# Large transfers of a two-layer SSM and MLP gradient kernel moved to other places in their queues

## The chip, the cores and the metric

The kernel runs on one core of one Trainium2 chip. A core has five engines that run their own instruction streams in order: PE (matrix multiplies; PEld is its weight load), DVE (vector), ACT (scalar and table functions), POOL and SP. Transfers between the device memory and the on-chip memory are issued by SP, ACT and POOL, each into a queue of its own, and are carried by 16 DMA engines that all queues share. SP does nothing in this kernel but issue transfers.

The metric is the time of one launch on the device in microseconds. Five runs of the kernel before gave 790.87 to 794.15 us, median 792.38 us.

## The reference, cut to what matters

The sequence has S = 2048 positions and D = 448 features, the inner width of the dense block is F = 1792, and all data are bfloat16. The kernel returns the output and eight gradients.

```
def A(q, k, v, shift_k, ssm_k, ssm_D):          # SSM convolution block
    kv = causal_conv4(k, shift_k) * v
    y  = irfft(rfft(kv, 4096) * rfft(ssm_k, 4096))[:2048] + kv * ssm_D
    return q * y
def B(x, w1, w2):                               # dense block
    return silu(x @ w1) @ w2

x = A_q
for layer in (0, 1):
    x = x + A(layernorm(x), A_k, A_v, A_shift_k, A_ssm_k, A_ssm_D)
    x = x + B(layernorm(x), B_w1, B_w2)
# outputs: x, and the gradients of sum(x * grad_out) with respect to
# A_q, A_k, A_v, A_shift_k, A_ssm_k, A_ssm_D, B_w1, B_w2
```

The convolution's result y does not depend on the layer, so it is computed once. The gradient that reaches y is summed over both layers and then goes back through the convolution once.

## The kernel before, in words

The program has three stages. `_ssm_prefix` computes y with a Fourier transform of 4096 points that is written as matrix products (a stage with the table M1, a transpose, a stage with a small table, and the inverse with the table Minv), and stores the spectra of the filter and of kv to the device memory (`SPEC_d["K"]`, `SPEC_d["KV"]`). `Main.run` does both layers forward and the dense blocks backward. `_ssm_suffix` takes the gradient back through the convolution and computes the gradients of the weights.

`Main.run` works on four chunks of 512 positions. Its first loop is the forward pass of layer 0. Its second loop does, for each chunk, layer 1 forward and backward; its third loop does layer 0 backward. For one chunk and half of F (seven tiles of 128), `h` makes the hidden activations `aT` (SiLU) and keeps the pre-activations `dT`, from which `slope` makes the derivative on ACT, in place, seven tiles in four instructions. `out` multiplies by w2 (`ps_o`). `ga` computes the gradient of the hidden layer in seven steps: `ps_g` on PE, a copy `ghp` on ACT out of PSUM, and a product with `dT` on DVE, which gives `ghT`. PSUM has two buffers for `ps_g`, so PE can be two steps ahead of ACT's copies and no more. `gn` multiplies by w1 (`ps_n`) and goes back through both layer norms, token tile by token tile: a copy `lb_u` on ACT, then a chain of vector instructions on DVE.

In layer 0, `dT` is stored to the device memory (`DT_d`) and is read back for the backward pass by `load_d` (L690), into tiles `dTl` of 896 KB that share three buffers with `dT`. The last chunk of the second loop loads the first one (`d0`), then `d1` and `e0`; the third loop loads the rest, each right after a transpose.

For the weight gradients, positions have to lie on the partitions, so `aT` and `ghT` are turned by transposing transfers from SP (`store_turned`, L484, two for each half of F, into a tile `turned` with two buffers) and the turned tiles are stored to `A_d` and `GH_d` by L486. That store is kept back in `self.late` until the next turn, and waits until its transposes have landed. Four blocks of layer 0's activations are stored untransposed in `AP_d` and are turned later by `turn_plain` (L496), in the second loop, one for each chunk.

`_ssm_suffix` starts with `_fft_stage1` (`ps_s` <- `gYb`, `M1s`; sixteen steps, copies `A1g` on ACT or DVE), then transposes (`ps_tr`), then seven spectrum steps of 2048 columns. In such a step `spectrum(cp)` loads the pieces of both stored spectra (`kk_c`, two buffers used in turn: K and KV, 512 KB each, from POOL's queue), transforms (`ps_s` <- `Zg`) and swaps halves by two transfers from ACT's queue (`xsw_c`, 256 KB each); `inverse(cp)` makes the products `pa` and `pb` on DVE and runs the inverse matmuls `ps_v`. `spectrum(cp + 1)` is issued ahead of `inverse(cp)`.

The weight gradients are 28 jobs each for w2 and w1: `_job` loads one `dstat` of 512 KB from SP's queue (L776) and does 16 matmuls `ps_d` with it against a big tile that stays: X and `GO` (grad_out) for w2, `mov3` and `mov1` for w1. These matmuls depend on little else, and the framework's scheduler lays them between the instructions of the other stages. The first three jobs' `dstat` are loaded while layer 0's backward pass starts.

The order of instructions on each engine is written out by the framework's scheduler when the program is built. `high_priority` brings an instruction forward, and `issue_after(x)` holds what is issued under it behind x. A tile with a `tag` shares its memory with the others of that tag in a pool, and waits for the release of the one before it. Tags that the change touches are: `WA` (w1sb, then `GO`), `WB` (w2sb, then `mov3`), `Y` (Ysb, then `ksf`), `GY` (gYb, then `gks`), and `kk0` (M1s, then every second `kk_c`). The big tiles are 1792 KB each (`GO`, `mov3`, `ksf`, `gks`); the tables `M1s` and `Minvs` are 1024 KB each.

Of the kernel before, what the change touches and what calls it, by code (L numbers as in the profile page):

```python
# [11 lines left out]
BF16 = mybir.dt.bfloat16  # L12
# [5 lines left out]
P = 128  # L18
# [3 lines left out]
J = 16  # L22
# [226 lines left out]
def _pm(ap2d):  # L249
    return ap2d.rearrange("(p j) d -> p j d", j=J)  # L250
# [213 lines left out]
class Main:  # L464
# [97 lines left out]

    def h(self, c, L, nT, half, hold):
        nc, k = self.nc, self.k
        aT = self.td.tile([P, NF // 2, 512], BF16, name="aT", tag="T", bufs=3)
        dT = self.td.tile([P, NF // 2, 512], BF16, name="dT", tag="D", bufs=3)
        hold.append((aT, dT))
        for ft0, n, at in ((0, 2, 1), (2, 2, 0), (4, 2, None), (6, 1, None)) if half == 0 else ((7, 1, None), (8, 2, 1), (10, 2, 0), (12, 2, None)):
            ps = k.psum.tile([P, 2, 512], FP32, name="ps_h", tag="mm", bufs=2)
            self.contract(ps, self.w1sb, nT, ft0, n, at)  # L570
            o = ft0 - 7 * half
            a = aT[:, o:o + n, :]
            tm = dT[:, o:o + n, :]
            last = nc.scalar.activation(a, ps[:, 0:n, :], ACT.Silu)  # L574
            e = nc.scalar if o == 4 else nc.vector
            _copy(nc, e, tm, ps[:, 0:n, :])
            k.bal.add("act", 0.52 * n)
            k.bal.add(*(("act", 0.52 * n) if e is nc.scalar else ("dve", 0.6 * n)))
        if L == 1:
            if half == 1:  # L580
                with self.tc.issue_after(last.ins):
                    for _, d in hold:
                        self.slope(d)
        else:
            nc.gpsimd.dma_start(out=k.DT_d[c, half], in_=dT[:])
            self.store_turned(k.A_d[0], aT, c, half, ((0, 4), (4, 7)) if half == 0 else ((4, 7),))
            if half == 1:
                nc.gpsimd.dma_start(out=k.AP_d[:, :, 512 * c:512 * (c + 1)].rearrange("ft f s -> f ft s"), in_=aT[:, 0:4, :])
        if L == 1:
            self.store_turned(k.A_d[1], aT, c, half)  # L590

    def out(self, c, aT, last):
# [114 lines left out]
    def run(self):  # L707
# [21 lines left out]
        for c in range(4):  # L729
            gb, gT = self.g_pre(c, 1)  # L730
            self.h(c, 1, nT, 1, cur)
            if c < 3:
                na1 = self.a_fwd(c + 1, 2, None)
            self.out(c, cur, True)
            self.turn_plain(c)
            if c == 3:
                d0 = self.load_d(0, 0)
                self.slope(d0)
                k.GO = k.wk.tile([P, NT, D], BF16, name="GO", tag="WA")
                with self.tc.issue_after(k.d_load.ins):  # L740
                    nc.sync.dma_start(out=k.GO[:], in_=_pm(k.grad_out[0]))
            box = []
# [6 lines left out]
            else:  # L749
                d1, e0 = self.load_d(0, 1), self.load_d(1, 0)  # L750
                k.go_jobs = k.d_load
                nl = self.load_n(0)
# [3 lines left out]
        for c in range(4):  # L756
# [10 lines left out]
            if c < 3:  # L767
                with self.tc.issue_after(k.d_load.ins):
                    nl = self.load_n(c + 1)
        self.flush()  # L770

# [52 lines left out]
def _ssm_suffix(k):  # L824
# [7 lines left out]
    with ExitStack() as es:  # L832
        pool = lambda name: es.enter_context(tc.tile_pool(name=name, bufs=1, reuse_waits="tile"))
        sp0 = pool("sp0")
        k.M1sb = sp0.tile([P, 16, 2, P], BF16, name="M1s", tag="kk0")
        with tc.high_priority():
            nc.gpsimd.dma_start(out=k.M1sb[:].rearrange("p a c k -> p (a c k)"), in_=k.m1_h.ap())
        sp = pool("sspec")
# [3 lines left out]
        Z = sp.tile([P, NDH, P], BF16, name="Zg")  # L842
        k.mov3 = k.wk.tile([P, NT, D], BF16, name="mov3", tag="WB")
        ksf = k.yk.tile([P, J, D], BF16, name="ksf", tag="Y")
        B1k = A1[:].rearrange("p a c n s -> p (a c n s)").rearrange("p (q d) -> p q d", d=D)
        _load_minv(k, nc.gpsimd)
        for n2 in range(16):
            _fft_stage1(k, n2, k.gYb[:, n2, :], A1, psum)
        with tc.tile_pool(name="sspec2", bufs=1, reuse_waits="tile") as p1:
# [8 lines left out]
            def spectrum(cp):  # L858
# [4 lines left out]
                nc.gpsimd.dma_start(out=t[0], in_=k.SPEC_d["K"][:, lo:hi])  # L863
                nc.gpsimd.dma_start(out=t[1], in_=k.SPEC_d["KV"][:, lo:hi])
                if cp == 4:
                    nc.gpsimd.dma_start(out=k.mov3[:], in_=_pm(k.N_d[3][:]))
                if cp == 2:
                    nc.gpsimd.dma_start(out=ksf[:], in_=_pm(k.KS_d[:]))
                for u in range(2):
# [8 lines left out]
            def inverse(cp, t):  # L878
                for u in range(2):
                    ci = 2 * cp + u  # L880
                    o = slice(u * 1024, (u + 1) * 1024)
                    for spec_t, B1, cnd in ((t[1], B1k, True), (t[0], Z, False)):
# [5 lines left out]
                        _fft_inv_stage2_chunk(k, pa, pb, True, B1, ci, psum, cnd=cnd)  # L888

            prev = spectrum(0)  # L890
            for cp in range(NCI // 2):
# [4 lines left out]
        p2 = es.enter_context(tc.tile_pool(name="sp2", bufs=1, reuse_waits="tile"))  # L896
        gks = k.xg.tile([P, J, D], BF16, name="gks", tag="GY")
        gkh = p2.tile([P, 3, D], BF16, name="gkh")
        kx = p2.tile([P, 19, D], BF16, name="kx_s")
        nc.gpsimd.memset(kx[0:1, 0:3, :], 0.0)  # L900
        for h in range(2):
            sl = slice(8 * h, 8 * h + 8)
            nc.scalar.dma_start(out=gks[:, sl, :], in_=v_pm[:, sl, :])
        nc.scalar.dma_start(out=kx[:, 3:19, :], in_=k_pm)
# [126 lines left out]
```

## Time and profile before

The profiled execution took 791.43 us with a span of 789.6 us on the core, at a mean granted PE clock of 0.978. The median of the five runs is 0.95 us above it.

| what | before |
|---|---|
| median of 5 runs | 792.38 us |
| profiled execution, its span | 791.43 us, 789.6 us |
| PE busy | 723.1 us, 92% of the span |
| DVE, ACT, POOL busy | 65%, 56%, 13% |
| moved by DMA | 183.69 MB, mean 233 GB/s |
| stages, from the span's start | prefix to 104 us, layer 0 forward to about 232, layer 1 to 408, layer 0 backward to 527, suffix to the end |

In the profile's lines "L574" is a line of the kernel, "out<-in" names the tiles with the buffer numbers left out, and "SPq", "ACTq" and "POOLq" are the instructions that issue transfers. What stands behind "<-" in square brackets is the instruction whose end closed an engine's idle time; it is inferred from semaphores. The stages' borders above are read from the timeline of PE. The view of waits gives us in total, the number of times and the longest; the view by windows gives for each stretch its length, each engine's busy time (with instructions), the granted PE clock, the DMA engines' busy share, which can exceed 1 a little, and GB/s.

### The profile page before, as it was taken

The numbers are of one execution on the slowest core, as the hardware profiler recorded it, in microseconds if no ns is written. First come the engines' busy times: TensorE is split into PE (matmuls) and PEld (weight loads), VectorE is DVE, ScalarE is ACT, GpSimd is POOL, SyncE is SP. The second block draws the span as 40 slices with busy tenths as digits, with TensorE's granted clock in tenths as the row PEclk, the third lists the DMA queues.
The fourth block names the chain that finished last, engine by engine and source line by source line (L and its number), as shares of the span: only waits on it lengthen the run. The fifth ranks groups of instructions, "written<-read, shape, count | busy, mean of one in ns | idle before, by whom it ended". The sixth has DMA issues, their size and how long they took to land.

```text
span 789.6 us, 12745 instructions
## 1 busy us (share of the span) xinstructions
PE 723.1 (92%) x5025; PEld 379.4 (48%) x5025; DVE 515.3 (65%) x1056; ACT 440.6 (56%) x551; POOL 102.6 (13%) x169
## 2 busy tenths in 40 slices
PE   5999779999999999999987898996979999999995
PEld 4976434444443444434433443343556774545553
DVE  3789678788434977859457877986455625797110
ACT  4879777666566576876846766643536644000000
POOL 1133212222100000000000000010111123111111
PEclk9999899999999999999998999998989999999998
DMA  9359999999977879879997987996978776687650
GB/s 307 147 158 283 372 234 310 306 268 208 241 217 140 178 194 218 214 171 219 352 274 229 237 226 202 262 213 202 413 218 265 249 267 218 181 304 223 189 178 17
DMA packets 188889, 183.69 MB, mean 233 GB/s; under 512 B 135483, under 2 KB 164031, under 8 KB 187805
## 3 DMA queue, kind: packets, MB, share of 16 engines
q1 hardware_dynamic: 173664, 120.93, 59.3%
q0 software_dynamic: 12832, 53.92, 19.6%
q10 hardware_dynamic: 2332, 8.03, 3.3%
q8 instruction: 39, 0.64, 0.3%
q14 instruction: 22, 0.17, 0.1%
HBM read 76.50 MB, written 65.87 MB: 180 GB/s over the span
## 4 chain that ended last, share of the span: by engine, by line
PE 32%; DVE 20%; issue 18%; ACT 14%; DMA 11%; POOL 4%; SPq 0%; POOLq 0%; DVEq 0%; ACTq 0%
PE ps_o L598 6%; PE ps_h L518 6%; PE ps_d L778 5%; ACT ghp L625 3%; DVE dT L113 3%; PE ps_g L518 2%; DMA dTl<-DT_d 2%; PE ps_n L666 2%; DVE lb_junk L641 2%; DVE ghT L630 2%; DMA kk_c<-spec_KV 2%; PE ps_v L232 2%; PE ps_v L233 2%; DVE lb_u L652 2%; DMA turned<-ghT 2%
## 5 line engine op out<-in xcount | busy, mean ns | idle before, releaser
L778 PEld LDWEIGHTS <-dstat 128*128 128x128 bf16 x896 | 86.5, 99 | 85.5 <-issue 6.4
L518 PE MATMUL ps_g<-gT,w2T 128*128 128x512 bf16 (+1 forms) x448 | 100.7, 386 | 15.8 <-ACT ghp L625 15.2
L518 PE MATMUL ps_h<-nT,w1sb 128*128 128x512 bf16 (+1 forms) x448 | 103.9, 385 | 4.9 <-DVE dT L113 2.6
L666 PE MATMUL ps_n<-w1T,ghT 128*128 128x448 bf16 x448 | 93.2, 353 | 1.2 <-DVE ghT L630 0.3
L598 PE MATMUL ps_o<-w2sb,aT 128*128 128x448 bf16 x448 | 90.8, 353 | 0.7 <-ACT aT L574 0.7
L778 PE MATMUL ps_d<-mov,dstat 128*128 128x448 bf16 x448 | 87.2, 352 | 1.1 <-DMA mov<-N_d 1.1
L574 ACT ACTIVATE aT<-ps_h 128x1024 bf16<-128x1024 f32 (+1 forms) x64 | 58.3, 918 | 37.3 <-PE ps_h L518 28.8
L113 DVE CAST dT<-ps_h 128x1024 bf16<-128x1024 f32 (+1 forms) x56 | 59.3, 1065 | 25.9 <-ACT aT L574 25.6
L625 ACT CAST ghp<-ps_g 128x1024 bf16<-128x1024 f32 x56 | 56.5, 1009 | 30.5 <-DVE ghT L630 19.2
L518 PEld LDWEIGHTS <-w2T 128*128 128x128 bf16 (+1 forms) x448 | 36.3, 97 | 76.7 <-issue 46.2
L518 PEld LDWEIGHTS <-w1sb 128*128 128x128 bf16 (+1 forms) x448 | 36.3, 97 | 68.5 <-issue 40.5
L666 PEld LDWEIGHTS <-ghT 128*128 128x128 bf16 x448 | 41.6, 98 | 46.2 <-DVE ghT L630 5.8
L598 PEld LDWEIGHTS <-aT 128*128 128x128 bf16 x448 | 42.1, 98 | 43.3 <-issue 4.3
L778 PE MATMUL ps_d<-X,dstat 128*128 128x448 bf16 x224 | 53.6, 369 | 4.2 <-DMA dstat<-A_d 4.2
L804 ACT COPY do<-ps_dt 112x512 bf16<-112x512 bf16 x14 | 8.2, 586 | 82.6 <-PE ps_dt L802 82.6
L232 PE MATMUL ps_v<-Gsb,pa 128*128 128x128 bf16 x336 | 42.8, 221 | 9.8 <-DVE Zg L113 5.5
L778 PE MATMUL ps_d<-GO,dstat 128*128 128x448 bf16 x224 | 49.5, 353 | 0.0
L233 PE MATMUL ps_v<-Gsb,pb 128*128 128x128 bf16 x336 | 41.7, 221 | 1.4 <-DVE pb L443 1.2
L819 DVE CAST dout<-ps_d 128x448 bf16<-128x448 f32 x14 | 8.7, 622 | 51.4 <-PE ps_d L778 51.4
L232 PEld LDWEIGHTS <-pa 128*128 128x128 bf16 x336 | 33.2, 99 | 12.2 <-DVE pa L442 6.5
L668 ACT ACTIVATE lb_u<-ps_n,rstd 128x448 f32<-128x448 f32 x32 | 20.3, 633 | 33.1 <-DVE X L653 12.1
L630 DVE TENSOR_TENSOR ghT<-dT,ghp 128x1024 bf16<-128x1024 bf16 (+1 forms) x32 | 19.5, 619 | 27.6 <-ACT ghp L625 27.6
(188 smaller groups left out, 1184.2 us busy)
## 6 DMA issues: line engine op xcount, KB each, us to landing
GH_d<-turned SPq DMA_DIRECT2D x16, 896.0 KB, 5.6
dstat<-A_d SPq DMA_DIRECT2D x28, 512.0 KB, 6.6
dstat<-GH_d SPq DMA_DIRECT2D x28, 512.0 KB, 3.8
A_d<-turned SPq DMA_DIRECT2D x12, 896.0 KB, 4.8
DT_d<-dT POOLq DMA_DIRECT2D x8, 896.0 KB, 6.4
dTl<-DT_d SPq DMA_DIRECT2D x8, 896.0 KB, 6.3
spec_K<-Z POOLq DMA_DIRECT2D x7, 512.0 KB, 7.7
KB<-Z POOLq DMA_DIRECT2D x14, 256.0 KB, 12.0
```

The source lines that it names most:

```text
L113: eng.tensor_copy(out, in_)
L232: nc.tensor.matmul(pv[:, i, :], lhsT=pa[:, i * P:(i + 1) * P], rhs=k.Gsb[:, ga, :], start=True, stop=False)
L233: nc.tensor.matmul(pv[:, i, :], lhsT=pb[:, i * P:(i + 1) * P], rhs=k.Gsb[:, gb, :], start=False, stop=True)
L518: self.nc.tensor.matmul(ps[:, u, :], lhsT=w[lo:hi, b, f:f + P], rhs=x[lo:hi, b, :], start=(seen[u] == 1), stop=(seen[u] == ND))
L574: last = nc.scalar.activation(a, ps[:, 0:n, :], ACT.Silu)
L598: nc.tensor.matmul(po[:, :D], lhsT=aT[ft // 7][0][:, ft % 7, tl * P:(tl + 1) * P], rhs=self.w2sb[:, ft, :], start=(ft == 0), stop=(ft == N ...
L625: k.last_gh = nc.scalar.copy(gh[:], ps[:])
L630: nc.vector.tensor_tensor(out=ghT[hh][:, o:o + len(u), :], in0=dT[hh][1][:, o:o + len(u), :], in1=gh[:, u[0]:u[0] + len(u), :], op=ALU.mult)
L641: nc.vector.scalar_tensor_tensor(out=junk[:], in0=u0, scalar=1.0, in1=n_t, op0=ALU.mult, op1=ALU.mult, accum_out=cp[:, 1:2])
L666: nc.tensor.matmul(pn[:, :D], lhsT=ghT[ft // 7][:, ft % 7, tl * P:(tl + 1) * P], rhs=self.w1T[:, ft, :], start=(ft == 0), stop=(ft == NF - 1))
L668: last_u = nc.scalar.activation(u0[:], pn[:, :D], ACT.Identity, scale=k.rstd[2 * L + 1][:, t:t + 1], accum_out=cp[:, tl, 0:1])
L778: i = k.nc.tensor.matmul(ps[:, :D], lhsT=st[:, t, :], rhs=mov[:, t, :], start=start and t == 0, stop=stop and t == NT - 1)
```

## The change

Nothing is computed differently. Transfers change their place, their queue, their number of pieces or their buffer.

- `d0`, the first `dTl`, is loaded at the start of `h(3, 1, ..., 1)` through the new argument `pre`, and no longer after `out(3)`. In SP's order it now stands behind the transposes of chunk 2's last `ghT` and ahead of chunk 3's last transposes. Its slopes move in ACT's order from behind chunk 3's activations to between chunk 2's `lb_u` copies.
- `turn_plain` runs twice in chunks 0 and 1 of the second loop, and not in chunks 2 and 3.
- `GO` is loaded in chunk 0 of the third loop, behind `load_n(1)`, and no longer in chunk 3 of the second.
- `M1s` is loaded by SP in chunk 2 of the third loop, into the tag `WB`, and no longer by POOL at high priority into `kk0`. `kk0` is then free for `kk_c` from the start.
- `mov3` had been loaded on POOL as soon as w2sb was free; it now follows `M1s` in `WB` and is loaded behind the spectra of step 5.
- `Minvs`, `ksf` and `gks` are loaded on POOL behind the spectra of steps 2, 3 and 4. `gks` had been two transfers on ACT's queue behind stage 1, and is now one.

As the scheduler sees other ready times, the order on PE, DVE, ACT and POOL changes too between about 355 us and the end of the spectra: the copies and matmuls of stage 1 start among layer 0's last `ps_n`, and the two `kk_c` pairs of steps 0 and 1 come ahead of the other large loads.

```
-    def h(self, c, L, nT, half, hold):
+    def h(self, c, L, nT, half, hold, pre=None):
...
         hold.append((aT, dT))
+        d0 = pre() if pre else None
...
+        return d0
...
         for c in range(4):
             gb, gT = self.g_pre(c, 1)
-            self.h(c, 1, nT, 1, cur)
+            d0 = self.h(c, 1, nT, 1, cur, (lambda: self.load_d(0, 0)) if c == 3 else None)
...
             self.out(c, cur, True)
-            self.turn_plain(c)
+            if c < 2:
+                self.turn_plain(2 * c)
+                self.turn_plain(2 * c + 1)
             if c == 3:
-                d0 = self.load_d(0, 0)
                 self.slope(d0)
-                k.GO = k.wk.tile([P, NT, D], BF16, name="GO", tag="WA")
-                with self.tc.issue_after(k.d_load.ins):
-                    nc.sync.dma_start(out=k.GO[:], in_=_pm(k.grad_out[0]))
...
                 d1, e0 = self.load_d(0, 1), self.load_d(1, 0)
+                k.GO = k.wk.tile([P, NT, D], BF16, name="GO", tag="WA")
...
             if c < 3:
                 with self.tc.issue_after(k.d_load.ins):
                     nl = self.load_n(c + 1)
+                    if c == 0:
+                        nc.sync.dma_start(out=k.GO[:], in_=_pm(k.grad_out[0]))
+                    if c == 2:
+                        k.M1sb = k.wk.tile([P, 16, 2, P], BF16, name="M1s", tag="WB")
+                        nc.sync.dma_start(out=k.M1sb[:].rearrange("p a c k -> p (a c k)"), in_=k.m1_h.ap())
...
         sp0 = pool("sp0")
-        k.M1sb = sp0.tile([P, 16, 2, P], BF16, name="M1s", tag="kk0")
-        with tc.high_priority():
-            nc.gpsimd.dma_start(out=k.M1sb[:].rearrange("p a c k -> p (a c k)"), in_=k.m1_h.ap())
...
-        k.mov3 = k.wk.tile([P, NT, D], BF16, name="mov3", tag="WB")
...
-        _load_minv(k, nc.gpsimd)
...
-                nc.gpsimd.dma_start(out=t[1], in_=k.SPEC_d["KV"][:, lo:hi])
-                if cp == 4:
-                    nc.gpsimd.dma_start(out=k.mov3[:], in_=_pm(k.N_d[3][:]))
-                if cp == 2:
-                    nc.gpsimd.dma_start(out=ksf[:], in_=_pm(k.KS_d[:]))
+                kv = nc.gpsimd.dma_start(out=t[1], in_=k.SPEC_d["KV"][:, lo:hi])
+                with tc.issue_after(kv.ins):
+                    if cp == 2:
+                        _load_minv(k, nc.gpsimd)
+                    if cp == 3:
+                        nc.gpsimd.dma_start(out=ksf[:], in_=_pm(k.KS_d[:]))
+                    if cp == 4:
+                        nc.gpsimd.dma_start(out=gks[:], in_=v_pm)
+                    if cp == 5:
+                        nc.gpsimd.dma_start(out=k.mov3[:], in_=_pm(k.N_d[3][:]))
...
+            gks = k.xg.tile([P, J, D], BF16, name="gks", tag="GY")
+            k.mov3 = k.wk.tile([P, NT, D], BF16, name="mov3", tag="WB")
             prev = spectrum(0)
...
-        gks = k.xg.tile([P, J, D], BF16, name="gks", tag="GY")
...
-        for h in range(2):
-            sl = slice(8 * h, 8 * h + 8)
-            nc.scalar.dma_start(out=gks[:, sl, :], in_=v_pm[:, sl, :])
         nc.scalar.dma_start(out=kx[:, 3:19, :], in_=k_pm)
```

## The prediction

> **What bounds the kernel now.** I read the page's busy times first: PE is busy 723.1 of 789.6 us, so a change can win only what PE spends idle or at a low clock. The waits of PE from 330 to 640 us come next. They name three places, and the waits of DVE (570 to 660 us, the last two lines) name a transfer behind the third.
>
> ```profile
> PE ps_g L518 <- ACT ghp L625: 14.3, 11, 7.1
> PE ps_v L232 <- DVE Zg L113: 5.5, 1, 5.5
> PE ps_d L778 <- DMA dstat<-A_d: 4.2, 1, 4.2
> PE ps_s L212 <- ACT A1g L111: 2.0, 1, 2.0
> ...
> DVE pb L886 <- DMA xsw_c<-Zg: 14.7, 6, 4.6
> ...
> DVE pa L885 <- DMA kk_c<-spec_KV: 5.9, 1, 5.9
> ```
>
> The chain that ended last, from 400 to 600 us, runs through a transfer at each of the three. These are its long pieces:
>
> ```profile
> 409.54 5.67 DMA dTl<-DT_d
> ...
> 521.49 13.24 DMA turned<-ghT
> 535.17 5.87 DMA dstat<-A_d
> ...
> 557.56 16.68 DMA kk_c<-spec_KV
> ```
>
> The view by windows shows what a stall does afterwards. After the length stand the busy times of PE, PEld, DVE, ACT and POOL, then granted clock, DMA share and GB/s. The first three stretches lie behind or in the three stalls and run at 0.50; the fourth holds the end of a 2.06 us gap and stays at 1.00. Then come the stretches ahead of and between the stalls, and the spectra.
>
> ```profile
> 416.40:423.20 6.80, 4.40 (x16) 1.48 (x15) 6.20 (x16) 6.21 (x10) 0.00 (x0) 0.50 0.66 257
> 539.30:546.10 6.80, 5.02 (x14) 2.11 (x15) 1.99 (x3) 0.91 (x1) 0.00 (x0) 0.50 0.60 236
> 573.40:580.20 6.80, 3.40 (x10) 1.49 (x11) 4.35 (x7) 0.00 (x0) 0.00 (x0) 0.50 0.78 217
> 476.20:480.20 4.00, 1.94 (x11) 0.91 (x11) 2.76 (x8) 4.00 (x6) 0.00 (x0) 1.00 0.99 341
> ...
> 375.00:397.00 22.00, 20.49 (x110) 8.98 (x108) 10.53 (x20) 18.62 (x21) 1.08 (x2) 1.00 1.05 348
> 519.00:541.00 22.00, 15.77 (x81) 7.63 (x79) 15.91 (x46) 7.81 (x15) 2.18 (x4) 0.96 1.01 252
> 580.30:636.00 55.70, 55.54 (x604) 39.93 (x603) 34.73 (x56) 35.78 (x40) 8.07 (x15) 1.00 0.71 227
> ```
>
> The DMA engines are full (1.05, 1.01) ahead of the first two stalls, and PE has no idle time in the spectra (55.54 of 55.70), where the share is 0.71. The timelines of SP and POOL show which transfers fill the engines:
>
> ```profile
> 376.47 0.57 SPq L741 DMA_DIRECT2D GO<-in_grad_out_dram  x1
> 390.80 8.34 SPq L484 DMA_TRANSPOSE turned<-ghT  x2
> ...
> 383.74 0.54 POOL L866 DMA_DIRECT2D mov<-N_d  x1 [37.07 <-PE ps_o L598]
> 519.05 0.54 POOL L837 DMA_DIRECT2D M1s<-c_m  x1
> 549.16 0.54 POOL L868 DMA_DIRECT2D ksf<-KS_d  x1 [10.01 <-DVE gYb L679]
> ```
>
> **The change part by part.** The profiled execution took 791.43 us, 0.95 below the median. Sums are against it.
>
> *First stall, 411.69 to 418.80 us.* `e0` was issued at 409.54 and landed 5.67 later; ACT waited 6.9 for it, with a `ghp` copy queued behind, and PE with the third `ps_g` behind that. `e0` is late because on SP it stands behind two pairs of transposes and `d1`. Without `GO` and `mov3` (3584 KB from 376 to 393) the first transpose should go out at about the 2 us of its neighbours with an idle queue, instead of 6.8, and the pair then ends with its data, near 395; `d1` goes at 395, not 399.23. From one `dTl` issue over the next pair to the next `dTl` issue took 10.3 to 11.5 us (399.23 to 409.54, 458.46 to 469.91), so `e0` goes at 405.8 and lands at 411.5, 3.8 earlier. ACT's new order has one slope more (0.95) ahead of the first `ghp`, so PE resumes 2.85 earlier. Some 4 us of stall are left, between the 2.06 gap that kept the clock and the 5.51 one that lost it. Before, the half clock cost (423.2 - 418.8) / 2 = 2.2; I count half of it as won. Part: -4.0. Ends: 0, where the pair is as slow as before, and -9.3, all of it.
>
> *The early `d0`.* Issued at 355.2 with a landing like `e0`'s, it is there at 360.9. ACT gets to it at 358.41 + 1.28 (table load) and waits 1.2; the second `lb_u` is 2.8 late, behind it DVE's norm chain and the copy of `gT`, and PE waits some 1.5 us for that copy at 366. In return the first `ghp` (387.24) loses a slope with a 1.24 wait, three slopes and two table loads ahead of it and comes about 0.75 earlier. 0; ends -1 and +2.5.
>
> *Plain blocks.* One more transpose (2.6 to 3.2 us of SP) and a store in chunks 0 and 1, behind which one `gb` load and the `ghT` transposes are queued. SP was idle 6.3 and 7.9 us there, and `gb` is used 30 us later. 0; the end without cover is +1.
>
> *Second stall, 533.80 to 541.08.* PE idled 1.95 and 4.23 us and then ran at half clock until 546.1, which cost (546.1 - 541.08) / 2 = 2.5: together 8.7. The fifth `dstat` waited on SP for the last store and this for the last pair of transposes, which went out in 9.5 us and landed at 534.7 beside `M1s` and `Minvs` (2048 KB). With `M1s` there since about 508, PE's new order needs the fifth `dstat` only 39 `ps_d` (0.186 each) and 22 `ps_s` (0.20) after the last `ps_n`: 11.7 us, against 35 and 6 before, 7.7 us. It came 14.1 us after; a last transpose of 1.5 instead of 5.9 makes that 9.7. The stall goes; late next is stage 1 behind DVE, whose norm chain of some 4.7 us a token tile now has seven 1.09 us copies in between: I leave 1.2 us. Part: -7.5; ends -8.7, and -3 where `kk_c` (also 1024 KB on POOL, where `Minvs` was) slows the transposes alike.
>
> *Third stall, 571.29 to 576.80.* 5.51 us and (580.2 - 576.8) / 2 = 1.7 of half clock. DVE waited for a KV piece that took 16.68 us with `ksf`, `gks` and four `kk_c` pieces in flight. Now both `kk_c` pairs are ahead and the big tiles behind. Late next is DVE's own copy `Zg`, 1.2 us after a `ps_s` that ended at 570.7, so 0.9 stay. Part: -6.3; ends -7.2 and -3. Two store issues wait on POOL behind the first `kk_c`; their tile has two buffers and its third user comes 16 us later: 0. ACT's two `gks` issues (1.0) lay in idle time: 0.
>
> *`GO` and `M1s` on SP in layer 0's backward pass.* Two issues of 0.57, behind `nb` and `na`, ahead of a store and the next transposes. SP had 8.8 and 3.2 us idle there. `GO` took 8.2 to land, `M1s` 11.5. +0.5; ends 0 and +3.
>
> *Four loads in the spectra.* Where they go, PE is full and nothing needs them for 30 us, but they share engines with what does. A step takes 8.4 us at a share of 0.71. The software queue moved 53.9 MB in 19.6% of the span, 2.9 us a MB at full share, so 1.8 MB more in each of three steps and 1.0 in one ask 18.8 us of the 16 engines, where about 0.29 x 50 = 14.5 are free. The `dstat` buffers, five deep, can lag. What is near is `xsw_c`: DVE's `pb` ends 2.6 to 2.9 us before PE wants it in steps 2, 3 and 5, but 0.2 to 0.4 in step 4 and 0.7 in step 6, and DVE waited for `xsw_c` already (14.7 us in all). With a big tile half landed I add 2 us to each: about 1.8 in step 4, 1.3 in step 6, some for the others. +3.5; ends 0, and +8, where the excess of 4.3 and the half clock after two stalls (3.4) all fall on PE.
>
> A page speaks against this part. The Trainium skill, "DMA: Bandwidth & Descriptors", section "Where 436 GB/s comes from", holds that transfers between HBM and SBUF are bound near 358 GB/s for a core. A step would ask 4.1 MB, which by that page is an estimated 11.5 us for each of three steps, and this part would be +9.4 and the whole sum -7.9. The row of 375 to 397 us has 348 GB/s, but at a share of 1.05 with transposes in it, so I stay with the row's shares.
>
> Sum: -4.0 + 0 + 0 - 7.5 - 6.3 + 0.5 + 3.5 = -13.8: 777.6, and with the 0.95 of the median 778.6.
>
> **The rivals.**
> *The first stall stays* (nothing there but a load moved). `e0` still needs both pairs of transposes and `d1`, and the second pair waits for `ghT` anyway. For it: neighbouring pairs without big loads took 5.8 to 7.2 us. Against: the first transpose at 390.80 took 6.8 alone. Sum without the 4.0: 782.6.
> *The spectra become the transfers' bound*, at +8 and with the second stall at its -3: 791.4 + 0.95 - 4.0 - 3 - 6.3 + 0.5 + 8 = 787.6.
> *Slower: the KV pieces of steps 4 to 6 land like the 16.68 us piece*, not in their median 7.2, as each follows a big tile in its queue. That is 9.5 late, against 4.2 to 4.8 us by which DVE's first product is ahead of PE, so 4.7 to 5.3 of stall each and 1.7 of half clock: +20 for three. With -17.3 for the rest, 795. It decides from some 6.6 us a step, stall and clock together. Against: then four pieces and two big tiles were out at once, now one pair and one tile.
> *No change.* The waits won come back at the next shared limit, as PE's order is fixed: 792.
>
> **How the numbers follow.** The forecast with all three stalls mostly gone has 0.55 (771 to 784 its own range), the first rival 0.2, the second 0.1, the slower one 0.1, no change 0.05. A measurement of this kernel cannot tell less than 0.3%, 2.4 us, from no change. The first three are faster: 0.85; same 0.05; slower 0.10. With the three stalls fully gone and the spectra at 0 the sum would be about -24, 768. The range goes from there over the second rival: 768 to 790.
>
> **What would show it.** Right: no gap over 2 us near 530 to 570, no 0.50 clock between the prefix and the end but perhaps near 415; the pair of transposes at about 390 under 6 us; `e0` issued by 406; the first two KV pieces landed before stage 1 ends. Wrong: PE waiting for `pa`, `pb` or `dstat` in steps 3 to 6, a DMA share at 1 there, or ACT idle long at 360 for `d0`. A new order of PE that puts a wait where none was, such as `ps_s` on DVE's norm chain, would undo the second part.

## The result, and the profile after

The changed kernel is slower, by 0.8%. It took 799.02 us (median of 25 runs, 794.69 to 818.93) against 793.54 us (44 runs, 786.79 to 814.98); the ratio is 1.0084, with a 95% interval of 1.0064 to 1.0105. Some executions of every kernel fall into a slower state, and the ratios leave these out, so a ratio is not the quotient of the two medians. The forecast was 778.6 us, in a range of 768 to 790, with 0.10 on slower. All ratios below are against runs of the kernel before on the same chip.

The profiled execution has a span of 793.8 us, 4.2 more than before, and PE is busy 726.6 us instead of 723.1. In the changed kernel and those made from it line numbers stand some 2 to 20 higher, and in after the spectra's products `pa` and `pb` are L891 and L892. PE's waits from 330 to 640 us, of after:

```profile
PE ps_g L518 <- ACT ghp L627: 10.9, 13, 3.9
PE ps_v L232 <- DVE Zg L113: 6.2, 3, 2.5
PE ps_v L233 <- DVE pb L892: 4.9, 3, 1.7
PE ps_s L212 <- ACT A1g L111: 3.6, 1, 3.6
```

And what DVE waited for from 560 to 660 us:

```profile
DVE pb L892 <- DMA xsw_c<-Zg: 24.3, 6, 7.6
DVE pb L892 <- PE ps_s L879: 6.8, 1, 6.8
```

The wait of 7.1 us for `ghp` is down to 3.9, the 4.2 us for `dstat` are gone, and one `ps_v` wait of 5.5 us has become three of at most 2.5. New are three waits of `ps_v` for `pb`, and DVE's waits for the half swap went from 14.7 to 24.3 us. The second line is by all signs one more of them: that `pb` starts at 593.23 us, and the second half of its swap landed at 593.11. The transfers in the chain that ended last, 400 to 640 us, are now all in the spectra and in front of them, apart from the last:

```profile
547.20 9.22 DMA kk_c<-spec_KV
...
571.48 8.02 DMA xsw_c<-Zg
...
604.46 12.12 DMA xsw_c<-Zg
...
638.34 9.15 DMA out_dram<-gK
```

The view by windows of after (length; busy PE, PEld, DVE, ACT, POOL; clock, DMA share, GB/s) first shows the three stretches at half clock in the spectra, and then the stretch that had held the large loads and three that together are the spectra:

```profile
582.50:589.30 6.80, 5.39 (x27) 3.13 (x27) 3.25 (x5) 1.93 (x2) 1.59 (x3) 0.50 0.99 328
606.30:609.80 3.50, 3.50 (x21) 2.21 (x20) 2.82 (x5) 1.81 (x3) 0.98 (x2) 0.51 1.05 366
620.00:626.80 6.80, 5.83 (x28) 3.33 (x28) 3.50 (x5) 1.93 (x2) 0.00 (x0) 0.50 0.33 83
375.00:397.00 22.00, 21.83 (x122) 9.96 (x121) 12.13 (x24) 14.96 (x17) 0.54 (x1) 1.00 0.83 202
...
575.00:600.00 25.00, 21.00 (x194) 14.07 (x192) 11.03 (x17) 10.99 (x12) 4.05 (x8) 0.86 1.01 346
600.00:622.00 22.00, 15.89 (x145) 10.62 (x142) 10.21 (x16) 9.16 (x10) 1.60 (x3) 0.88 0.88 286
622.00:640.00 18.00, 17.98 (x177) 12.38 (x176) 6.94 (x13) 10.16 (x11) 4.57 (x5) 0.87 0.53 158
```

The engines of the transfers were relieved where the loads came from (1.05 to 0.83) and are full where they went: 1.01 for 25 us, where the whole stage had 0.71 before. PE, which had no idle time there, now loses 1.44 (ahead of 580.37), 2.52 (583.91), 1.70 (604.97), 1.72 (617.44) and 2.52 us (620.98), 9.9 in all, and half of its busy time in the three stretches at half clock, (5.39 + 3.50 + 5.83) / 2 = 7.4. The spectra cost 17.3 us more.

POOL's timeline shows which loads these gaps stand behind:

```profile
566.89 0.53 POOL L205 DMA_DIRECT2D Minvs<-c_minv  x1
...
573.74 0.53 POOL L870 DMA_DIRECT2D ksf<-KS_d  x1
...
588.30 0.54 POOL L872 DMA_DIRECT2D gks<-in_A_v_dram  x1 [1.90 <-issue]
...
598.87 0.53 POOL L874 DMA_DIRECT2D mov<-N_d  x1
```

The whole account, from the two profiles (gaps and half clock together):

| place | forecast | profile |
|---|---|---|
| first stall | -4.0 | 3.91 us and no half clock, for 9.3: -5.4 |
| second stall | -7.5 | 3.56 us and no half clock, for 8.7: -5.1 |
| third stall | -6.3 | 1.16 us, for 7.2: -6.0 |
| spectra | +3.5 | +17.3 |
| w1's first turns, 702 to 709 us | not in it | 2.21 us and half clock, less what before lost there: about +3 |
| sum | -13.8 with `GO` at +0.5 | about +4, and the span says +4.2 |

One profile is one draw. In seven further profiles below whose layers are those of after, the first gap was 4.6 to 5.7 us, each time with half clock behind it (1.7 to 1.9 us), so that stall usually won about 2 us and not 5.4. The second gap was 3.6 to 5.6 in six of them; the seventh changes what stands there.

### The profile page after: what moved, and what is told of

It is laid out like the page before. It is cut to its first block, busy times and chain, and to the rows that moved or that the text cites. A ratio compares the mean times of both kernels' runs of the same rounds, so it can differ in the third digit from the quotient of the medians.

```text
span 793.8 us, 12744 instructions
## 1 busy us (share of the span) xinstructions
PE 726.6 (92%) x5025; PEld 382.9 (48%) x5025; DVE 515.5 (65%) x1056; ACT 440.2 (55%) x551; POOL 102.8 (13%) x169
## 4 chain that ended last, share of the span: by engine, by line
issue 41%; PE 21%; DVE 14%; DMA 9%; ACT 9%; POOL 4%; SPq 0%; POOLq 0%; ACTq 0%; DVEq 0%
PE ps_h L518 5%; PE ps_o L600 4%; PE ps_d L784 3%; DVE dT L113 3%; DMA xsw_c<-Zg 3%; ACT na L274 2%; PE ps_v L232 2%; PE ps_v L233 1%; DVE ln_st L260 1%; DMA KB<-Z 1%; POOL out_dram L811 1%; DMA kk_c<-spec_KV 1%; DMA out_dram<-gK 1%; PE ps_cv L370 1%; ACT A1K L111 1%
## 5 line engine op out<-in xcount | busy, mean ns | idle before, releaser
L518 PE MATMUL ps_g<-gT,w2T 128*128 128x512 bf16 (+1 forms) x448 | 98.9, 381 | 12.4 <-ACT ghp L627 11.8
L784 PE MATMUL ps_d<-mov,dstat 128*128 128x448 bf16 x448 | 88.9, 357 | 0.6 <-DMA mov<-N_d 0.6
L232 PE MATMUL ps_v<-Gsb,pa 128*128 128x128 bf16 x336 | 45.3, 227 | 10.7 <-DVE Zg L113 6.2
L784 PE MATMUL ps_d<-GO,dstat 128*128 128x448 bf16 x224 | 54.1, 379 | 0.0
L784 PE MATMUL ps_d<-X,dstat 128*128 128x448 bf16 x224 | 50.9, 355 | 0.0
L233 PE MATMUL ps_v<-Gsb,pb 128*128 128x128 bf16 x336 | 44.1, 228 | 6.2 <-DVE pb L892 4.9
L233 PEld LDWEIGHTS <-pb 128*128 128x128 bf16 x336 | 33.7, 102 | 17.7 <-DVE pb L892 6.1
L892 DVE TENSOR_TENSOR pb<-xsw_c,kk_c 128x1024 bf16<-128x1024 bf16 x28 | 19.0, 685 | 31.1 <-DMA xsw_c<-Zg 24.3
```

The lines of the kernel that those rows point to most:

```text
L232: nc.tensor.matmul(pv[:, i, :], lhsT=pa[:, i * P:(i + 1) * P], rhs=k.Gsb[:, ga, :], start=True, stop=False)
L233: nc.tensor.matmul(pv[:, i, :], lhsT=pb[:, i * P:(i + 1) * P], rhs=k.Gsb[:, gb, :], start=False, stop=True)
L518: self.nc.tensor.matmul(ps[:, u, :], lhsT=w[lo:hi, b, f:f + P], rhs=x[lo:hi, b, :], start=(seen[u] == 1), stop=(seen[u] == ND))
L784: i = k.nc.tensor.matmul(ps[:, :D], lhsT=st[:, t, :], rhs=mov[:, t, :], start=start and t == 0, stop=stop and t == NT - 1)
L892: nc.vector.tensor_tensor(out=pb[:], in0=t[2][:, o], in1=spec_t[:, o], op=ALU.mult)
```

## The experiments

**First four: which part does what.** The theory was that the half swaps, which DVE needs within 3 us of slack, are late because large tiles use the same 16 engines beside them. The rivals were PE's new order of filler work, late KV pieces, and one single load, `mov3`.

`four`: before, with only the four loads of the suffix moved as in after.

```
-        _load_minv(k, nc.gpsimd)
...
+                with tc.issue_after(kv.ins):
+                    if cp == 2: _load_minv(k, nc.gpsimd)
+                    if cp == 3: ... ksf   # 4: gks, 5: mov3
```

> The kernel before with one part alone: Minvs, ksf, gks and mov3 behind the KV pieces of steps 2 to 5. M1s stays on POOL, the layers stay as they were. Theory 1: the stall at 571 us (5.5, and 1.7 of half clock) goes, and steps 2 to 5 lose about what they lost in the changed kernel (9.9 of gaps and 7.4 of half clock): ratio 1.005 to 1.015. Rival: with the old filler order there are no gaps in the spectra, and the ratio is 0.985 to 0.992.

Measured: 795.75 us, ratio 1.002 (0.9981 to 1.0059). DVE's waits of this kernel, 555 to 645 us:

```profile
DVE pb L889 <- DMA xsw_c<-Zg: 26.8, 5, 7.3
...
DVE pa L888 <- DMA kk_c<-spec_KV: 0.2, 1, 0.2
```

The stalls of the spectra are there (2.53, 2.89, 2.67 and 2.43 us), and one of 2.69 us behind a swap stands where the third stall was. PE does 132 filler products ahead of the first `ps_v` here, for 135 in before and 121 in after, so the stalls do not need after's order of PE; the KV pieces, at 0.2 us, are not the late ones. The ratio is under the theory's 1.005 to 1.015; the first stall, which it had left as it was, is down to 3.64 us although `GO` is at its old place.

`layers`: after's layers with before's suffix, so `mov3` is loaded early again and `GO` late.

> The changed kernel's part in the layers alone (early d0, plain blocks two a chunk, GO in layer 0's backward pass), with the suffix of the kernel before: mov3 again early on POOL, M1s and Minvs on POOL before stage 1. If GO alone filled the engines ahead of the first transposes of chunk 3's ghT, the pair takes under 6 us and the wait for e0 is about 4 us as in the changed kernel: 4 to 5 us won, ratio 0.994. If mov3 alone is enough to hold them up, the first transpose still takes over 5 us and nothing is won, ratio 1.000. The stalls at 537 and 571 us stay in both cases.

Measured: 790.89 us, ratio 0.9964 (0.9923 to 1.0005). No gap over 1 us in the spectra, and the first stall is 7.81 us with half clock until 423.7. Moving `GO` alone won nothing there: of the two loads that the prediction took together, the profiles of `four` and `layers` leave `mov3`.

`nomov`: after, with `mov3` alone taken out of the spectra, to behind the clearing of `gkh`.

> The changed kernel with only mov3 taken out of step 5 and loaded on POOL behind the spectra. Theory 1: the gaps of step 2 (1.4 and 2.5) and step 4's first stay, those of step 5 (1.7 and 2.5) and their half clock go: some 7 us less than the changed kernel, ratio 0.998 to 1.003. Rival (order of PE): no difference to the changed kernel, 1.008.

Measured: 800.24 us, ratio 1.008 (1.0037 to 1.0123), as after. One tile less in the spectra was worth nothing in time, against the 7 us that the theory forecast; where they went this run doesn't show. `late`, the next one, has `mov3` at the same place and a new stall behind the spectra.

`late`: all four loads out of steps 2 to 5: `Minvs` and `ksf` behind step 0's pair, `gks` behind the last half swap on ACT's queue, `mov3` as in `nomov`.

> The changed kernel with the four loads taken out of spectrum steps 2 to 5: Minvs and ksf behind the KV piece of step 0, gks on ACT's queue behind the last half swap, mov3 on POOL behind the spectra. PE's order keeps its new form. Theory 1 (the half swaps xsw_c land late because the 1.8 MB tiles share the DMA engines with them): xsw_c back at a median landing near 4 us instead of 7.5, at most 2 us of PE waits in steps 1 to 6, no 0.50 clock between 560 and 640 us, and the gains at 410, 523 and 558 kept: some 15 us under the kernel before, ratio 0.978 to 0.985. Rival (PE's new order leaves too few filler matmuls ahead of the products, whatever is loaded): the same 1.4 to 2.5 us gaps in steps 2, 4 and 5 and the half clock after them, ratio 1.00 to 1.01.

Measured: 797.6 us, ratio 1.0057 (1.0023 to 1.0091). In steps 1 to 6 one gap over 1 us is left (1.25). But PE's waits from 560 to 670 us are

```profile
PE ps_v L233 <- DVE pb L890: 8.4, 2, 7.2
PE ps_r L930 <- ACT gK L111: 6.0, 1, 6.0
```

The stall went with the loads: 7.2 us in step 0, whose swap landed 13.6 us after it was asked for, with `Minvs` and `ksf` in flight, and 6.0 us behind the spectra, where the copy of `gK` waited for stores that ran beside `mov3`, `gks` and `kx_s`. So steps 2 to 5 are not the matter: at both new places, too, something with little slack stood beside the tiles.

**Second four: how much, and in what size.** `spread` cuts the loads: `Minvs` in halves at steps 2 and 3, `ksf` in quarters at steps 0, 4, 5 and 6, `gks` behind the last swap on ACT's queue, `mov3` behind the last store of `ksf`.

```
-                    if cp == 2: _load_minv ... 5: mov3
+                    if cp in (2, 3):
+                        _load_minv_half(k, nc.gpsimd, cp - 2)
+                    if cp in (0, 4, 5, 6):
+                        q = max(0, cp - 3)
+                        nc.gpsimd.dma_start(out=ksf[:, 4 * q:4 * q + 4, :], in_=_pm(k.KS_d[:])[:, 4 * q:4 * q + 4, :])
```

> After, with its four loads cut small: the constants of Minvs in two halves of 512 KB behind the KV pieces of steps 2 and 3, ksf in four pieces of 448 KB behind those of steps 0, 4, 5 and 6, gks on ACT's queue behind the last half swap, mov3 on POOL's queue behind the last store of ksf. Theory of shares (a half swap is late when large tiles pass through the engines beside it): at most 0.5 MB more per step leaves the share of the transfer engines in the spectra under about 0.85; the five stalls of after there (9.9 us, and some 7 us of half clock) shrink to 3 us or less, PE's second run of layer 1 keeps what after has won, and the span is 778 to 784 us (ratio 0.985, range 0.977 to 0.995). Rival, the load's bytes count and not their size: the four loads still ask for the same bytes in the same stage, the stalls only spread over more steps, and the time is that of after within 0.4% (ratio 1.004 to 1.012).

Measured: 784.64 us, ratio 0.9914 (0.9874 to 0.9954): faster than both kernels, in the range of the theory of shares. The spectra have gaps of 1.16 and 1.62 us and no half clock. The longest landing of one half of a swap is 7.1 us, for 12.1 in after.

`spread_d0`: `spread` with the early `d0` undone.

> The same kernel with the early load of layer 1's first difference undone (asked for again after the fourth chunk of layer 2's last pass). What the early load is worth by itself: the prediction put it at 0 (-1 to +2.5). If the early load helps, the first transposed products start 2 to 3 us later than in spread and the time is 2 to 3 us above it; if its wait on ACT costs, the gaps of 0.6 and 1.1 us in front of them go and the time is 1 to 2 us below it.

Measured: 786.75 us, ratio 0.9951 (0.9911 to 0.9991). That is 2.1 us above `spread`, and the spans differ by 2.3, but the intervals overlap: the early `d0` may be worth some 2 us, and the runs don't settle it.

`spread_kk0`: `spread` with all loads of K and KV held behind the last store of `G`.

```
+                with tc.issue_after(k.g_out.ins):
                     nc.gpsimd.dma_start(out=t[0], in_=k.SPEC_d["K"][:, lo:hi])
```

> The same kernel with every load of a K and KV pair held behind the last store of layer 1's outputs, so that the first pair doesn't run beside the last transposes. If the first pair is what makes those transposes late, the gap of about 3.6 us at the second half's 14th or 15th block (about 522 to 526 us in after) shrinks under 1 us, and the gap ahead of the first spectra grows by up to 4 us, since four pairs (4 MB) are then asked for in one go; the time is within 3 us of spread. If the transposes are late by themselves (9.9 us for a pair on SP's queue), the gap stays at 3 to 4 us.

Measured: 786.09 us, ratio 0.9938 (0.9911 to 0.9966). The gap ahead of 529 us shrank from 3.62 to 1.35 us, and the one ahead of the first `ps_v` grew from 1.26 to 3.24: as expected, the first pair beside the last transposes is a good part of the second stall, and here the gain went into the next one.

`noload`: after, but `ksf`, `gks` and `mov3` are not loaded, zeros stand in their place (POOL writes them), and the four outputs that use them, the gradients of k, v, shift_k and w1, lack these terms.

> After, but it leaves out the loads of ksf, gks and mov3 (zeros in their place, so the three outputs that add them lack their terms); Minvs is loaded as in after. Theory of shares: the stalls of spectra steps 3 to 6 and of the stage behind go, that of step 2 (Minvs) stays: about 13 to 17 us under after, ratio 0.98 to 0.985. Rival, the new order of PE's filler work behind the spectra causes the stalls: they stay, and the time is within 3 us of after (ratio 1.004 to 1.012).

Measured: 788.67 us, ratio 0.998 (0.9944 to 1.0016). That is about 1% under after and so less than the 13 to 17 us I expected. The spectra's part was as expected in kind: with `Minvs` alone in it the stage has gaps of 2.53 (step 2) and 1.92 us and 3.4 us at half clock, 6.2 us in all for 17.3. But this profile lost 5.4 us in the first stall with half clock, and 2.1 in the tail.

`pieces`: after with all four loads in pieces of 448 or 512 KB over steps 1 to 6, so the same 6.4 MB in the stage.

```
+                    if cp in (2, 3): _load_minv_half(...)
+                    if cp in (1, 4, 5, 6): ... a quarter of ksf
+                    if cp in (2, 3, 4, 5): ... a quarter of gks
+                    if cp in (3, 4, 5, 6): ... a quarter of mov3
```

> After, with the same four loads at the same steps of the spectra or one beside them, but each cut into pieces of 448 or 512 KB: Minvs in two at steps 2 and 3, ksf in four at steps 1, 4, 5, 6, gks in four at steps 2 to 5, mov3 in four at steps 3 to 6. All bytes of after are asked for in the same stage (6.4 MB); only the size of one transfer changes. If the size of a transfer that stands ahead of a half swap makes it late, the stalls of the spectra shrink to about those of spread (under 4 us of gaps, no half clock) and the time is 784 to 790 us (ratio 0.988 to 0.997). If the bytes make it late, the gaps stay at 8 us or more and the ratio at 1.004 to 1.012.

`whole`: `spread` with `Minvs` and `ksf` in one piece each, at steps 2 and 3.

> The kernel spread with Minvs and ksf loaded whole (1024 KB behind the KV piece of step 2, 1792 KB behind that of step 3, as after has them); gks and mov3 stay outside the spectra as in spread. If the size of one transfer counts, the gaps of after at 578 to 584 us and at 603 us come back (4 to 6 us with half clocks behind them) and the time is 5 to 9 us above spread (ratio 0.997 to 1.003). If the bytes of the stage count, it is as spread within 2 us, since the bytes are the same.

Measured: `pieces` 798.0 us, ratio 1.007 (1.0037 to 1.0103), `whole` 789.63 us, 0.9945 (0.9915 to 0.9976). The size of a piece alone is not it: cut small, the same bytes cost what they cost in after (gaps of 3.17, 1.75, 2.53, 1.66 and 2.53 us between 565 and 629). `whole` lies between its two expectations, some 2.5 us above `spread` by the ratios, whose intervals overlap. Where the swap was beside the whole `ksf` the gaps of 1.48 and 2.53 us are back, with half clock behind them, and elsewhere in the spectra there is none. So what counts is how many bytes go beside one swap; a large piece is one way to put them there.

What a swap shares the engines with can be counted from the packets in the traces: over the 119 swaps of before, after and the kernels of this study (without `nomov`), the time from asking for a swap's first half to the landing of both, by the bytes that the queues of POOL and SP moved meanwhile:

| moved beside it | swaps | us, median (least to most) |
|---|---|---|
| under 0.3 MB | 25 | 4.3 (4.1 to 5.6) |
| 0.3 to 0.7 | 26 | 4.4 (4.2 to 7.4) |
| 0.7 to 1.2 | 26 | 6.6 (4.9 to 9.0) |
| 1.2 to 1.8 | 18 | 7.5 (6.2 to 10.9) |
| 1.8 to 2.5 | 17 | 8.5 (7.3 to 9.2) |
| 2.5 and more | 7 | 12.9 (10.0 to 17.5) |

A line through them is 4.0 us and 2.5 us for a MB (correlation 0.92). A longer transfer has more beside it in any case, so this table alone is no proof; the runs above, which set the bytes, are. It gives the size, though: with the 2.6 to 2.9 us of slack of steps 2, 3 and 5, a swap may have about 1 MB beside it. One pair of K and KV is 1 MB.

**What sets the first stall.** `e0pool` is `spread` with `e0` asked for on POOL's queue, when its buffer is free, and not behind the transposes on SP's. `epool` does so with the like loads of the third and fourth chunk too.

```
-                d1, e0 = self.load_d(0, 1), self.load_d(1, 0)
+                d1, e0 = self.load_d(0, 1), self.load_d(1, 0, nc.gpsimd)
```

> The kernel spread with one load more moved: the difference e0 of layer 1's second chunk is asked for on POOL's queue, where its buffer comes free at about 397 us, and not on SP's behind the second pair of layer 2's last transposes (402.7 us in spread). If the rest of the first stall is those transposes on the queue, the 5.3 us gap at 408 us goes, and its half clock, and the time is 4 to 8 us below spread; if the load itself then lands late beside them, the gap shrinks by less than 2 us.

> As e0pool, and the like load of layer 1's third and fourth chunk on POOL's queue too (in spread they stand behind 8 us of transposes on SP's and end gaps of 3.5 us at 438 us and 1.9 us at 473 us). By the same reason both gaps go: 6 to 14 us below spread, ratio to before 0.974 to 0.984. If the transposes slow down beside the loads, what is won comes back as later transposes: within 3 us of e0pool.

Measured: `e0pool` 792.25 us, ratio 1.0005 (0.9972 to 1.0038); `epool` 804.64 us, 1.0114 (1.0073 to 1.0155). Both are worse than `spread`, and the gains that their first cases forecast did not come. In `e0pool` the load was asked for at 398.1 us and took 11.5; in `spread` it was asked for at 402.7 and took 6.0, and landed a little earlier. The gap grew from 5.26 to 8.81 us, and most of that is not the load: ACT's order changed too. In `spread` ACT does four slope instructions ahead of its wait for `e0`, and the first `ghp` copy starts 3.5 us after the landing; in `e0pool` all eight stand between the landing and that copy, which starts 8.0 us after it. In `epool` the view of transfers has

```profile
dTl<-DT_d SPq DMA_DIRECT2D x5, 896.0 KB, 6.2
...
dTl<-DT_d POOLq DMA_DIRECT2D x3, 896.0 KB, 14.1
```

and SP's timeline a pair of transposes beside the last of these loads:

```profile
464.13 20.12 SPq L488 DMA_TRANSPOSE turned<-ghT  x2
```

Such a pair took 8.0 us in `spread`. A load beside a pair of transposes makes both slow, and asking for it earlier won nothing. What that costs in the first gap is not separated from ACT's order; the last gap of `epool`, 7.98 us ahead of 487 us, stands behind a load that landed 18.1 us after it was asked for.

**Two things open then.** The bytes had been changed in each run that relieved the spectra, and the first stall had no cause that held. `ahead` keeps all loads of after and makes the half swaps, with the products in front of them, one step further ahead, in three buffers.

```
-            prev = spectrum(0)
+            xs = [spectrum(0), spectrum(1)]
             for cp in range(n):
+                if cp + 1 < n: kks.append(load_kk(cp + 1))
+                if cp + 2 < n: xs.append(spectrum(cp + 2))
```

> After with the half swaps (and the stage-2 products in front of them) made one step further ahead, in three buffers where there were two; the loads of K and KV and the four moved loads stay at their steps, with all their bytes. If it is the lateness of the swap alone that costs, the DVE's waits for the swap (24.3 us in after) fall under 5 us, the gaps of 9.9 us in the spectra go, with most of the half clock, and the time is 10 to 16 us under after (ratio 0.988 to 0.996). If the bytes slow the step otherwise (the K and KV pieces become the late ones, or DVE's reads), the gaps stay in part, with another name at their end, and the time is less than 6 us under after.

Measured: 792.27 us, ratio 0.9998 (0.9971 to 1.0024), some 0.9% or 7 us under after, between the two expectations. DVE's waits, 550 to 645 us:

```profile
DVE pa L894 <- DMA kk_c<-spec_KV: 23.0, 5, 8.8
...
DVE pb L895 <- DMA xsw_c<-Zg: 1.4, 1, 1.4
```

The swap is waited for no more, and the KV pieces are in its place: gaps of 2.91 and 3.66 us, ahead of 606.78 and 620.48, with half clock behind each, cost 12.5 us by the same count as the 17.3 of after. So the slack of the swap was only a part of the cause. The rest is that steps 3 to 5 ask for more than the engines give: from 586 to 622 us the share is 1.02 to 1.03.

`anch5` is `spread` with one order changed on ACT: the slope of `e0` (and of the next chunks' `e`) is held behind the fifth of a chunk's seven `ghp` copies, where it had stood ahead of the third.

```
-            if fp == 2 and mid:
+            if fp == (2 if L else 5) and mid:
...
+                with self.tc.issue_after(k.last_gh.ins):
                     self.slope(e0)
```

> The kernel spread with one order changed on ACT: the slope of the difference e of the next chunk stands between the fifth and the sixth of a chunk's copies of the gradient products, and no longer ahead of the third; loads and transposes stay as they are. If PE waits for copies that stand behind the slope, the gaps of 5.3 us (408 us), 3.5 us (438 us) and 1.9 us (473 us) go or fall under 1 us each, with their half clocks, and the time is 7 to 14 us under spread (ratio to before 0.974 to 0.985). If the slope is then late for the next chunk, gaps of the same size come about 10 us later, and the time is that of spread within 2 us.

Measured: 785.32 us, ratio 0.9904 (0.9866 to 0.9942), as `spread`. PE's waits from 400 to 480 us in `spread`, and then, 390 to 560 us, in `anch5`:

```profile
PE ps_g L522 <- ACT ghp L631: 11.2, 5, 5.3
```

```profile
PE ps_s L216 <- ACT A1g L111: 5.9, 1, 5.9
PE ps_g L522 <- ACT ghp L631: 5.0, 11, 1.4
```

The three gaps of layer 0's backward pass (5.26, 3.52 and 1.86 us) went, down to one of 1.44, and no half clock is left there. So PE had waited for copies that stood behind a slope that stood behind a late load; the load may be late if nothing that PE needs is queued behind it. But nothing was won in the time: PE came to the end of stage 1's cover 9 us earlier and stood there for 5.9 us, and two swaps stalled again (1.81 and 2.53, 1.54 and 2.52 us).

`both` is `anch5` with the swaps one step further ahead, and `both_kk0` holds the K and KV loads behind the last store of `G` as well.

> The kernel anch5 with the half swaps one step further ahead, as in ahead: 0.5 MB of moved loads a step, and a step more of slack for the swap. If bytes beside a transfer with little slack are the whole cause, PE has no gap over 1 us between the first and the last of the spectra (anch5 has 8.4 us of them and 5 us of half clock), and the time is 6 to 11 us under anch5 (774 to 780 us, ratio 0.977 to 0.985). If the K and KV pieces become late as in ahead, two gaps of 2 to 4 us stay, and the time is within 3 us of anch5.

> The same with the K and KV loads held behind the last store of layer 1's outputs. If the first pair makes the last transposes late, the 5.9 us gap at 517 us of anch5 shrinks to 3 us or less; the pairs that are then asked for in one go may cost up to 3 us ahead of the first spectra. Against both: -3 to +2 us.

Measured: `both` 780.23 us, ratio 0.9852 (0.9818 to 0.9886); `both_kk0` 773.82 us, ratio 0.9769 (0.9733 to 0.9806), the fastest of all, 3.1% under the changed kernel by the two ratios. In `both` one gap is left in the spectra (2.29 us, no half clock), where I expected none over 1; it is a K and KV pair, and the time is just short of the 774 to 780 us expected. `both_kk0` won 6.6 us more, against an expectation of -3 to +2: the copy `A1g`, which waited for the last transposes in after, `spread`, `anch5` and `both`, has no gap of PE behind it any more. PE's waits in `both_kk0`, 400 to 700 us:

```profile
PE ps_g L522 <- ACT ghp L631: 5.0, 11, 1.4
PE ps_v L236 <- DVE pa L903: 3.8, 1, 3.8
PE ps_s L888 <- DVE Zg L113: 2.0, 1, 2.0
```

One stall of 3.8 us is left, in the spectra and with half clock behind it, and what DVE's `pa` waits for there is again a KV piece.

## Why the prediction was wrong

*"Four loads in the spectra" failed; the rest was of the right sign.* It was put at +3.5 with ends 0 and +8, and measured about +17. The step that failed is the sum by mean shares: 18.8 us asked, 14.5 free, and the 4.3 of excess at the worst all on PE. Bytes don't wait for a free place. Each tile was asked for 4 to 10 us ahead of the swap of its own step and was still landing beside it, and what was asked for behind the swap took its share at once as well, so these four swaps were 4 to 8 us late against 0.2 to 2.9 of slack, and the share that was free later in the stage (0.53 from 622 us) was of no use. The mechanism had been named (`xsw_c` is what is near) and its price, "2 us to each", was wrong. The right row was in the trace of before: the halves of its swaps landed in 3.7 us in the median and 8.1 at the most, and the swap asked for at 570.1 us, beside the pieces of two pairs of K and KV, took 8.7 by the count above.

*The half clock.* I counted it for two stalls, 3.4 us. There were three stretches, 7.4 us.

*The Trainium skill's rule* in "DMA: Bandwidth & Descriptors", section "Where 436 GB/s comes from", which holds a core's transfers between HBM and SBUF to about 358 GB/s, was weighed and set aside. The spectra of after ran at 346 GB/s at a share of 1.01, near that figure; but the kernel before moved 416 GB/s from 552 to 568 us, at the same share and with transfers to and from the device memory alone, so the figure is no bound in this case. By the estimate from it this part would have been +9.4: nearer than mine and still short, since it too counts only the excess.

*First stall, -4.0:* the profile has -5.4, but its usual value in kernels with the same layers is about -2. That a transfer ahead was the cause is half right: without `mov3` the stall is shorter, `GO` has no part in it, and what holds PE is ACT's order, as `anch5` shows. The step "`e0` is late because on SP it stands behind two pairs of transposes" was wrong as a reason: taken from behind them, it was as late (landed at 409.6 us, for 408.7). What the forecast said of the pair itself came true in after: the pair at 388 us went out in 4.8 us, and `e0` was asked for at 403.75.

*Second stall, -7.5 with an end of -3 "where `kk_c` slows the transposes alike":* -5.1 in the profile, less in the others. That end is what happened: the last pair went out in 9.9 us, beside the first K and KV pair, and ACT's copy `A1g` waited for its landing (4.8 us), presumably for memory that the turned tile gives up. In `both_kk0`, with that pair later, the gap is gone. The wait for `dstat` is gone as forecast; DVE's norm chain, which the forecast had as late next, cost 0.2 us.

*Third stall, -6.3:* -6.0. Right, by the reason given.

*Early `d0`, 0:* between 0 and -2, not settled. *Plain blocks and `GO` on SP:* nothing in the profile speaks of them.

*Not in it:* about 3 us at 702 to 709 us, where a `dout` copy of DVE stood behind its products and additions for the gradient of k. PE had done fewer filler products ahead of the spectra (121 for 135), and the order behind them shifted; that is seen in the two traces and was not tested.

*The rivals.* That the spectra become the transfers' bound had 0.1 and 787.6 us; it had the right place, with a price of +8, which is half of what was measured. The signs named for being wrong, PE waiting for `pb` and a share of 1 in the spectra, are what came. The one on the slower side named the KV pieces of steps 4 to 6; in after their waits are not among DVE's longest, and they were late only in `ahead`, `both` and `both_kk0`, once the swaps had slack. A rival in which the half swaps are late was not listed, though the text had its slack in numbers.

## What to carry to other kernels

When loads are moved into a stage, don't compare their bytes with its mean free share: take every small transfer that something waits for there, its slack, and the longest time that the trace shows for it beside a large load. Either give that transfer a step more of slack or keep the loads beside it under what the slack allows, and then look which transfer is the next; here fewer bytes a step gave 0.9% (`spread`), more slack or ACT's order alone only moved the stall, and all three with the later K and KV loads gave 2.3% (`both_kk0`). An in-order engine that does a late load's work ahead of copies that others need turns that load's lateness into their stall: change the order there before the transfer.

## What the runs showed of the hardware

- Transfers of different queues share the engines, and a later one does not wait for an earlier one to end. In after the swap asked for at 583.9 us took 9.2 us; of the 2.3 MB that moved beside it, 1.4 MB were the K and KV pieces and `gks`, asked for 1.4 to 4.4 us behind it on POOL's queue, and 0.4 MB were the end of `ksf`, asked for 10 us ahead of it.
- Transposing transfers and plain loads slow each other: 896 KB took 6.2 us behind a pair of transposes and 14.1 beside one, and a pair of transposes 20.1 us for 8.0.
- PE's half clock came in stretches of 3.4 us and multiples of it (3.4 and 6.8 in after, but for the last, which the end of the program cuts), and the gap's length did not decide alone. In after, gaps of 1.70 (ahead of 604.97 us) and 1.94 us (ahead of 471.88) were followed by half clock, and gaps of 3.91 (413.75) and 3.56 us (526.07) were not.
